# Linformer attention and an MLP mixer on one core: gated loads, reordered transposes, and stores on ScalarE's queue

## The chip, the cores and the metric

The kernel runs on one core of a Trainium2 chip. A core has a matrix engine (TensorE, in the profile PE; its weight loads are PEld), a vector engine (VectorE, DVE), an engine for activations (ScalarE, ACT), a general one (GpSimd, POOL) and SyncE (SP), which here only issues DMAs. Each engine works through its own instructions in order and waits at an instruction until the semaphores that it names are there. A DMA is issued by SP, ACT or POOL, and its data then move on DMA engines that all of them share. The metric is the device time of one execution in microseconds (us).

## What is computed

Eight batches, eight heads, 1024 positions, 64 values per head. Keys and values are first projected from 1024 positions to 64 (Linformer), then come scores, softmax and the weighted sum. The heads put side by side give x of 1024 x 512 per batch, which goes through a token-mixing and a channel-mixing MLP.

```python
k_proj = np.einsum('ks,bhsd->bhkd', E, k)          # E: 64 x 1024
v_proj = np.einsum('ks,bhsd->bhkd', F, v)
scores = scale * np.matmul(q, k_proj.transpose(0, 1, 3, 2))
attn = softmax(scores)
x = heads side by side of np.matmul(attn, v_proj)  # b, 1024, 512
h = np.maximum(x.transpose(0, 2, 1) @ w_tok1, 0.0) @ w_tok2   # 1024 -> 256 -> 1024
u = x + h.transpose(0, 2, 1)
h2 = np.maximum(u @ w_ch1, 0.0) @ w_ch2            # 512 -> 1536 -> 512
return u + h2
```

## The kernel before

All matrices are held in bf16; products are summed in f32 in PSUM. GpSimd loads q, k and v (f32 in memory) and casts them on the way (`load_kv` L79, `load_q` L87, two DMAs of 512 KB for each of q, k, v from batch 1 on). The tiles `k_sb`, `v_sb` and `q_sb` have two buffers each, so a batch's tiles are those of the batch two before.

The work of a batch has two parts. The *front* (`front_units`) is a list of steps: `kv_proj` (L176, L177), `k_transpose` (L191), four `scores` (matmuls L202, exp on ACT L207), eight `attend` (matmuls L214, division on DVE L221 and L222), two `token1` (L232, relu on ACT L236) and eight `token2` (L241, add on DVE L245, which gives `u_sb`). After the fourth and the eighth `token2`, SP transposes a half of `u_sb` by DMA into `uT` (L248). `token1` and `token2` share one PSUM buffer, so the next `token2` waits until DVE has read the last.

The *back* (`back_blocks`) is channel mixing, cut into 48 blocks of four matmuls. `ch1` (24 blocks, L347) makes a chunk `g_ps` of the hidden layer from `uT`, and ACT's relu puts it into `gT` (L351). `ch2` (24 blocks, L358; three make one output tile) sums `o2_ps` from `gT`, which the profile calls `o_ps` like that of `attend`; DVE adds `u_sb` (L365) into an output tile `o_sb`, one of four, and SP stores it (L366, 256 KB). `g_ps` and `o2_ps` take turns in the three PSUM banks of `psC`. Batch 0 runs all `ch1` before all `ch2`; the others go half by half: 12 `ch1`, 12 `ch2`, 12 `ch1`, 12 `ch2`.

A loop over the batches weaves the back of batch b with the front of batch b + 1: after each block as many steps are emitted as keep the two lists in proportion. Batches 0 and 1 transpose q on PE (L161, `qT` by ACT, L166). From batch 2 on SP transposes it by DMA, two of them per batch (`q_transpose`, L95), and that step stands in the middle of the steps of the loop before: the loop of batch b transposes q of batch b + 2. At the loop's start GpSimd copies one element of `gT` into `gate` (L398), and behind it in the source come the loads of batch b + 2.

The source's order is not binding. A scheduler puts every engine's instructions in an order of its own, as their dependences allow; the copy to `gate` and the loads behind it share no data. The profile's times are those of the order so found.

Of the kernel before, what the change touches and what calls it, by code (L numbers as in the profile page):

```python
# [15 lines left out]
def kernel(  # L16
# [13 lines left out]
    nc = tc.nc  # L30
    P = 128

    B, H, S, D = q.shape
# [18 lines left out]
    attn_pool = ctx.enter_context(tc.tile_pool(name="attn", bufs=4))  # L52
    mix_pool = ctx.enter_context(tc.tile_pool(name="mix", bufs=2))
    gT_pool = ctx.enter_context(tc.tile_pool(name="gT", bufs=2))
    out_pool = ctx.enter_context(tc.tile_pool(name="outp", bufs=4))
    psC = ctx.enter_context(tc.tile_pool(name="psC", bufs=3, space=bass.MemoryType.PSUM))
    psA = ctx.enter_context(tc.tile_pool(name="psA", bufs=2, space=bass.MemoryType.PSUM))
    psS = ctx.enter_context(tc.tile_pool(name="psS", bufs=1, space=bass.MemoryType.PSUM))
# [11 lines left out]
    def load_kv(b, parts):  # L70
        k_sb, v_sb, q_sb = [
            kv_pool.tile([P, H, NSI, D], BF16, tag=name, name=name) for name in ("k_sb", "v_sb", "q_sb")
        ]
        qT = mix_pool.tile([P, H, NJ, P], BF16, tag="qT", name="qT")
        loaded[b] = (k_sb, v_sb, q_sb, qT)
        hn = H // parts
        for h in range(0, H, hn):
            for t, src in ((k_sb, k), (v_sb, v)):
                nc.gpsimd.dma_start(  # L79
                    out=t[:, h : h + hn],  # L80
                    in_=src[b, h : h + hn].rearrange("h (p si) d -> p h si d", p=P),
                )

    def load_q(b, parts):
        hn = H // parts
        for h in range(0, H, hn):
            nc.gpsimd.dma_start(  # L87
                out=loaded[b][2][:, h : h + hn],
                in_=q[b, h : h + hn].rearrange("h (p si) d -> p h si d", p=P),
            )  # L90

    def q_transpose(b):
        q_sb, qT = loaded[b][2:]
        for h in range(0, H, H // 2):
            nc.sync.dma_start_transpose(  # L95
                out=qT[:, h : h + H // 2].rearrange("p h j s -> p (h j) s"),
                in_=q_sb[:, h : h + H // 2].rearrange("p h si d -> p (h si d)"),
            )

    load_kv(0, HP)  # L100
# [7 lines left out]
    for c in range(0, DC, DC // 4):  # L108
        nc.gpsimd.dma_start(
            out=wc1_sb[:, :, c : c + DC // 4],  # L110
            in_=moe_w_ch1.rearrange("(dc p) c -> p dc c", p=P)[:, :, c : c + DC // 4],
# [4 lines left out]
    for c in range(0, CC, CC // 4):  # L116
        nc.gpsimd.dma_start(
            out=wc2_sb[:, c : c + CC // 4],
            in_=moe_w_ch2.rearrange("(cc p) d -> p cc d", p=P)[:, c : c + CC // 4],
# [24 lines left out]
    def front_units(b):  # L144
# [189 lines left out]
        units += [lambda si=si: token2(si) for si in range(NSI)]  # L334
        return units

    out_v = out.rearrange("b (p si) d -> b p si d", p=P)

    def back_blocks(b):

        u_sb, uT = us.pop(b), uTs.pop(b)
        st = {}

        def ch1(i, cc):
            g_ps = psC.tile([P, S2], F32, tag="c", name="g_ps")
            for dc in range(DMC):
                nc.tensor.matmul(  # L347
                    g_ps, wc1_sb[:, dc, cc * P : (cc + 1) * P], uT[i][:, :, dc, :],
                    start=(dc == 0), stop=(dc == DMC - 1),
                )  # L350
            nc.scalar.activation(out=st["gT", i][:, cc, :], in_=g_ps, func=ACT.Relu)  # L351

        def ch2(i, ss, part):
            if part == 0:
                st["o"] = psC.tile([P, DM], F32, tag="c", name="o2_ps")
            o2_ps = st["o"]
            for cc in range(part * 4, part * 4 + 4):
                nc.tensor.matmul(  # L358
                    o2_ps, st["gT", i][:, cc, ss * P : (ss + 1) * P], wc2_sb[:, cc, :],
                    start=(cc == 0), stop=(cc == CC - 1),  # L360
                )
            if part == CC // 4 - 1:
                si = i * NJ + ss
                o_sb = out_pool.tile([P, DM], F32, tag="o_sb", name="o_sb")
                nc.vector.tensor_add(out=o_sb, in0=o2_ps, in1=u_sb[:, si, :])  # L365
                nc.sync.dma_start(out=out_v[b, :, si, :], in_=o_sb)  # L366

        def half(i):
            st["gT", i] = gT_pool.tile([P, CC, S2], BF16, tag="gT", name="gT")

        up, down = [], []
        for i in range(2):
            up.append([lambda i=i: (half(i), ch1(i, 0))])
            up[i] += [lambda i=i, cc=cc: ch1(i, cc) for cc in range(1, CC)]
            down.append(
                [lambda i=i, ss=ss, p=p: ch2(i, ss, p) for ss in range(NJ) for p in range(CC // 4)]
            )
        if b == 0:
            blocks = up[0] + up[1] + down[0] + down[1]
        else:  # L380
            blocks = up[0] + down[0] + up[1] + down[1]
        return blocks, lambda: st["gT", 0]

    gate = const.tile([1, 1], BF16, name="gate")
    rest = front_units(0)
    for b in range(B):
        blocks, first_tile = back_blocks(b)
        n0, n1 = 2, len(blocks) - 5
        if b == 0:
            for block in blocks[:16]:  # L390
                block()
                if rest:
                    rest.pop(0)()
        else:
            blocks[0]()
        if b + 2 < B:

            nc.gpsimd.tensor_copy(out=gate, in_=first_tile()[0:1, 0, 0:1])  # L398
            load_kv(b + 2, 2)
            load_q(b + 2, 2)  # L400
        if b == 0:
            blocks = blocks[16:]
            n0, n1 = 0, len(blocks) - 4
        else:
            blocks = blocks[1:]
        units = front_units(b + 1) if b + 1 < B else []
        if b + 2 < B:
            units.insert(len(units) // 2, lambda b=b: q_transpose(b + 2))
        done = 0
        for n, block in enumerate(blocks):  # L410
            block()
            want = max(0, n + 1 - n0) * len(units) // (n1 - n0)
            while done < min(want, len(units)):
                units[done]()
                done += 1


# [1 line left out]
_INS = ['q', 'k', 'v', 'E', 'F', 'moe_w_tok1', 'moe_w_tok2', 'moe_w_ch1', 'moe_w_ch2']  # L419
_OUTS = [((8, 1024, 512), 'float32')]  # L420
# [25 lines left out]
```

## Time and profile before

| | us |
|---|---|
| median of 3 runs | 499.16 |
| lowest, highest | 493.22, 503.42 |
| the profiled execution | 492.7 |
| its span, first to last instruction | 490.9 |
| PE busy in it | 453.0 (92%) |
| DVE, ACT, POOL busy | 176.1, 165.9, 50.0 |

The granted TensorE clock is 0.981 on average. A row of the profile names the line of the kernel, the engine and what the instruction writes and reads (`out<-in`, buffer numbers left out, or with one where there are several of a name). Of a DMA the row of the issuing queue (SPq, POOLq) shows how long it held the queue; "to landing" is from issue to the last byte.

### The profile page before, as it was taken

To read this page: it belongs to the slowest core of one execution; us is meant where nothing else is said; L and a number is where in the kernel's file an instruction comes from. 1 tells how busy PE (TensorE), PEld (TensorE's weight loads), DVE (VectorE), ACT (ScalarE), POOL (GpSimd) and SP (SyncE) were. 2 spreads that over 40 slices of the span, in tenths; PEclk is the share of its full clock that TensorE was granted. 3 is DMA by queue.
4 is the path that set the end of the run, shared out by engine and by line. 5 is a ranking of instruction groups with operands and counts; after the bars stand their busy time and mean duration, and the time that the engine had idled before them with its cause. 6 is when DMAs were issued, how large, how long until landed. Compare 5 with 4: busy or idle time off the path is not lost.

```text
span 490.9 us, 6248 instructions
## 1 busy us (share of the span) xinstructions
PE 453.0 (92%) x2588; PEld 220.6 (45%) x2624; DVE 176.1 (36%) x345; ACT 165.9 (34%) x259; POOL 50.0 (10%) x78
## 2 busy tenths in 40 slices
PE   2789999249999999999999999999999999999996
PEld 2566444014444444444444444444454434444442
DVE  3472224113361534332452525243351425241102
ACT  1257560002525053322524062422524061514150
POOL 7533320110210020100200020000000000000000
PEclk9999999678999999999999999999999999999999
DMA  8999999999895459924980559223010601033102
GB/s 127 207 204 206 206 206 197 202 210 229 141 203 86 99 121 210 170 43 131 163 181 1 122 120 210 64 64 108 22 65 0 160 12 65 21 87 85 65 21 85
DMA packets 93051, 60.43 MB, mean 123 GB/s; under 512 B 56160, under 2 KB 84320, under 8 KB 93024
## 3 DMA queue, kind: packets, MB, share of 16 engines
q0 software_dynamic: 29728, 29.63, 37.1%
q1 hardware_dynamic: 63296, 30.42, 25.3%
q8 instruction: 20, 0.33, 0.3%
q14 instruction: 7, 0.06, 0.0%
HBM read 59.24 MB, written 16.78 MB: 155 GB/s over the span
## 4 chain that ended last, share of the span: by engine, by line
PE 76%; DMA 16%; SPq 5%; issue 1%; POOL 0%; DVE 0%; POOLq 0%; DVEq 0%
PE o_ps L358 30%; PE g_ps L347 30%; DMA wc_sb<-in_moe_w_ch_dram 7%; DMA q_sb<-in_q_dram 6%; PE u_ps L241 5%; SPq L95 5%; PE h_ps L232 4%; DMA out_dram<-o_sb 2%; PE o_ps L214 2%; PE kv_ps L176 2%; PE s_ps L202 2%; DMA v_sb<-in_v_dram 1%; PE kt_ps L191 0%; DVE o_sb L365 0%; POOL k_sb L79 0%
## 5 line engine op out<-in xcount | busy, mean ns | idle before, releaser
L351 ACT ACTIVATE gT<-g_ps 128x512 bf16<-128x512 f32 x192 | 115.2, 600 | 232.9 <-PE g_ps L347 232.5
L358 PE MATMUL o_ps<-wc_sb,gT 128*128 128x512 bf16 x739 | 182.3, 382 | 1.6 <-issue 0.2
L347 PEld LDWEIGHTS <-wc_sb 128*128 128x128 bf16 x768 | 72.2, 98 | 84.5 <-issue 5.8
L358 PEld LDWEIGHTS <-gT 128*128 128x128 bf16 x768 | 72.5, 98 | 80.1 <-issue 6.3
L365 DVE TENSOR_TENSOR o_sb<-o_ps,u_sb 128x512 f32<-128x512 f32 x64 | 44.3, 692 | 85.4 <-PE o_ps L358 66.8
L245 DVE TENSOR_TENSOR u_sb<-u_ps,x_sb 128x512 bf16<-128x512 f32 x56 | 38.7, 692 | 92.7 <-PE u_ps L241 90.8
L241 PE MATMUL u_ps<-hT_sb,wt_sb 128*128 128x512 bf16 x111 | 34.3, 390 | 17.5 <-DVE u_sb L245 17.5
L222 DVE TENSOR_TENSOR x_sb<-o_ps,rdn 128x512 bf16<-128x512 f32 x64 | 44.3, 692 | 2.2
L207 ACT ACTIVATE a_sb<-s_ps 128x1024 bf16<-128x1024 f32 x32 | 32.9, 1032 | 29.6 <-PE s_ps L202 29.5
L221 DVE RECIPROCAL rdn<-o_ps 128x8 f32<-128x8 f32 x64 | 13.1, 205 | 68.2 <-PE o_ps L214 68.2
L181 DVE CAST kp_sb<-kv_ps 64x512 bf16<-64x512 f32 (+1 forms) x22 | 10.9, 532 | 54.3 <-PE kv_ps L177 54.3
L241 PEld LDWEIGHTS <-wt_sb 128*128 128x128 bf16 x112 | 16.2, 145 | 30.9 <-issue 21.8
L214 PEld LDWEIGHTS <-a_sb 128*128 128x128 bf16 x256 | 19.5, 99 | 16.5 <-DVE x_sb L222 3.2
L232 PE MATMUL h_ps<-x_sb,wt_sb 128*128 128x512 bf16 x106 | 26.1, 379 | 0.4
L87 POOL DMA_DIRECT2D q_sb<-in_q_dram x18 | 13.3, 739 | 85.8 <-DMA qT<-q_sb 75.4
L176 PE MATMUL kv_ps<-k_sb,ET_sb 128*64 128x512 bf16 (+1 forms) x88 | 18.3, 355 | 3.8 <-DMA k_sb<-in_k_dram 3.8
L177 PE MATMUL kv_ps<-v_sb,FT_sb 128*64 128x512 bf16 (+1 forms) x88 | 17.4, 354 | 3.1 <-DMA v_sb<-in_v_dram 3.1
L398 POOL COPY gate<-gT 1x1 bf16<-1x1 bf16 x6 | 1.1, 177 | 155.7 <-ACT gT L351 155.7
L232 PEld LDWEIGHTS <-wt_sb 128*128 128x128 bf16 x112 | 11.0, 98 | 13.2
L236 ACT ACTIVATE hT_sb<-h_ps 128x512 bf16<-128x512 f32 x14 | 8.4, 597 | 25.0 <-PE h_ps L232 25.0
L79 POOL DMA_DIRECT2D k_sb<-in_k_dram x18 | 13.5, 752 | 27.6 <-PE kv_ps L177 20.3
L214 PE MATMUL o_ps<-vb_134,a_sb 128*128 128x130 bf16 x128 | 12.8, 223 | 2.3 <-DVE x_sb L222 2.3
(67 smaller groups left out, 342.4 us busy)
## 6 DMA issues: line engine op xcount, KB each, us to landing
out_dram<-o_sb SPq DMA_DIRECT2D x64, 256.0 KB, 2.6
k_sb<-in_k_dram POOLq DMA_DIRECT2D x14, 512.0 KB, 9.7
v_sb<-in_v_dram POOLq DMA_DIRECT2D x14, 512.0 KB, 11.6
q_sb<-in_q_dram POOLq DMA_DIRECT2D x14, 512.0 KB, 11.4
wc_sb<-in_moe_w_ch_dram POOLq DMA_DIRECT2D x8, 384.0 KB, 16.2
k_sb<-in_k_dram POOLq DMA_DIRECT2D x4, 256.0 KB, 7.6
v_sb<-in_v_dram POOLq DMA_DIRECT2D x4, 256.0 KB, 8.2
q_sb<-in_q_dram POOLq DMA_DIRECT2D x4, 256.0 KB, 10.0
```

Of the source, the lines that this page charges most:

```text
L95: nc.sync.dma_start_transpose(out=qT[:, h : h + H // 2].rearrange("p h j s -> p (h j) s"), in_=q_sb[:, h : h + H // 2].rearrange("p h si d ...
L176: nc.tensor.matmul(kv_ps[0:KP], ET_sb[:, si, :], k_sb[:, hs, si, :], start=a, stop=z)
L207: nc.scalar.activation(out=a_sb, in_=s_ps, func=ACT.Exp, scale=scale)
L214: nc.tensor.matmul(o_ps[:, j // 2, (j % 2) * 2 * D1 : (j % 2 + 1) * 2 * D1], a_sb[:, h % 2, j * P : (j + 1) * P], vb[:, h // 2, h % 2].rea ...
L222: nc.vector.tensor_tensor(out=x_sb[:, :, h * D : (h + 1) * D].rearrange("p (n c) d -> p n c d", n=2), in0=o4[:, :, :, 0:D], in1=rdn[:, :, ...
L232: nc.tensor.matmul(h_ps, wt1_sb[:, si, t * P : (t + 1) * P], x_sb[:, si, :], start=(si == 0), stop=(si == NSI - 1),)
L241: nc.tensor.matmul(u_ps, wt2_sb[:, t, si::NSI], hT_sb[:, t, :], start=(t == 0), stop=(t == TC - 1),)
L245: nc.vector.tensor_add(out=u_sb[:, si, :], in0=u_ps, in1=x_sb[:, si, :])
L347: nc.tensor.matmul(g_ps, wc1_sb[:, dc, cc * P : (cc + 1) * P], uT[i][:, :, dc, :], start=(dc == 0), stop=(dc == DMC - 1),)
L351: nc.scalar.activation(out=st["gT", i][:, cc, :], in_=g_ps, func=ACT.Relu)
L358: nc.tensor.matmul(o2_ps, st["gT", i][:, cc, ss * P : (ss + 1) * P], wc2_sb[:, cc, :], start=(cc == 0), stop=(cc == CC - 1),)
L365: nc.vector.tensor_add(out=o_sb, in0=o2_ps, in1=u_sb[:, si, :])
```

## The change

- `load_ahead` issues the copy to `gate` and ties the loads of batch b + 2 behind it (`tc.issue_after`): they can't be put ahead of it. In loop 0 the copy stands where it stood, behind the first 16 blocks; in later loops behind the sixth block, and it reads the sixth chunk of `gT`.
- The two DMA transposes of q are kept in the source's order on SP (`tc.keep_in_program_order`) and are appended to the steps, behind the last `token2` and so behind both transposes of u, where they stood in the middle.
- A store is no longer issued by SP with its add. It is put on a list and issued by ACT after the next block and the steps behind that one (`flush`); the rest follow at the end.
- The output tile has five buffers for four.
- The loops from batch 1 on spread their steps over 42 blocks where it was 40, since their first block is now part of the list.

```diff
-    out_pool = ctx.enter_context(tc.tile_pool(name="outp", bufs=4))
+    out_pool = ctx.enter_context(tc.tile_pool(name="outp", bufs=5))
...
     def q_transpose(b):
         q_sb, qT = loaded[b][2:]
         for h in range(0, H, H // 2):
-            nc.sync.dma_start_transpose(
-                out=qT[:, h : h + H // 2].rearrange("p h j s -> p (h j) s"),
-                in_=q_sb[:, h : h + H // 2].rearrange("p h si d -> p (h si d)"),
+            tc.keep_in_program_order(
+                nc.sync.dma_start_transpose(
+                    out=qT[:, h : h + H // 2].rearrange("p h j s -> p (h j) s"),
+                    in_=q_sb[:, h : h + H // 2].rearrange("p h si d -> p (h si d)"),
+                )
             )
...
+    stores = []
+
+    def flush(n):
+
+        for dst, o_sb in stores[:n]:
+            nc.scalar.dma_start(out=dst, in_=o_sb)
+        del stores[:n]
...
-                nc.sync.dma_start(out=out_v[b, :, si, :], in_=o_sb)
+                stores.append((out_v[b, :, si, :], o_sb))
...
+    def load_ahead(b, cc):
+
+        if b + 2 < B:
+            passed = nc.gpsimd.tensor_copy(out=gate, in_=first_tile()[0:1, cc, 0:1])
+            with tc.issue_after(passed.ins):
+                load_kv(b + 2, 2)
+                load_q(b + 2, 2)
...
-        n0, n1 = 2, len(blocks) - 5
         if b == 0:
-            for block in blocks[:16]:
+            for n, block in enumerate(blocks[:16]):
                 block()
                 if rest:
                     rest.pop(0)()
-        else:
-            blocks[0]()
-        if b + 2 < B:
-
-            nc.gpsimd.tensor_copy(out=gate, in_=first_tile()[0:1, 0, 0:1])
-            load_kv(b + 2, 2)
-            load_q(b + 2, 2)
-        if b == 0:
+            load_ahead(0, 0)
             blocks = blocks[16:]
-            n0, n1 = 0, len(blocks) - 4
-        else:
-            blocks = blocks[1:]
+        n0, n1 = (0, len(blocks) - 4) if b == 0 else (2, len(blocks) - 4)
         units = front_units(b + 1) if b + 1 < B else []
         if b + 2 < B:
-            units.insert(len(units) // 2, lambda b=b: q_transpose(b + 2))
+            units.append(lambda b=b: q_transpose(b + 2))
         done = 0
         for n, block in enumerate(blocks):
+            made = len(stores)
             block()
+            if b > 0 and n == 5:
+                load_ahead(b, 5)
             want = max(0, n + 1 - n0) * len(units) // (n1 - n0)
             while done < min(want, len(units)):
                 units[done]()
                 done += 1
+            flush(made)
+    flush(len(stores))
```

Line numbers of the changed kernel are 1 to 10 higher, so L96 below is L95 before, L250 is L248, and a store is L344.

On SP, the first instructions of the program, which belong to loop 0, stood before like this (`qT` of batches 2 and 3, `uT` of batch 1, and the stores of batch 0):

```order
L95 DMA_TRANSPOSE qT<-q_sb 128x16x128 x2
L366 DMA out_dram<-o_sb 128x512
L95 DMA_TRANSPOSE qT<-q_sb 128x16x128 x2
L366 DMA out_dram<-o_sb 128x512 x4
L248 DMA_TRANSPOSE uT_728<-u_sb 128x16x128
L366 DMA out_dram<-o_sb 128x512 x2
L248 DMA_TRANSPOSE uT_729<-u_sb 128x16x128
```

And after the change, on SP from the same place on (`uT` of batch 1, `qT` of batch 2, then `uT` of batch 2):

```order
L250 DMA_TRANSPOSE uT_728<-u_sb 128x16x128
L250 DMA_TRANSPOSE uT_729<-u_sb 128x16x128
L96 DMA_TRANSPOSE qT<-q_sb 128x16x128 x2
L250 DMA_TRANSPOSE uT_1131<-u_sb 128x16x128
L250 DMA_TRANSPOSE uT_1132<-u_sb 128x16x128
```

The stores are gone from SP, the transposes of u stand ahead of those of q, and those of batch 3 have left loop 0.

On GpSimd, the difference between loop 0 and loop 1, behind the loads of batch 2 (with `q_sb` at its head):

```order
 L87 DMA q_sb<-in_q_dram 128x4x512 x2
-L79 DMA k_sb<-in_k_dram 128x4x512
-L79 DMA v_sb<-in_v_dram 128x4x512
-L79 DMA k_sb<-in_k_dram 128x4x512
-L79 DMA v_sb<-in_v_dram 128x4x512
-L87 DMA q_sb<-in_q_dram 128x4x512 x6
-L398 COPY gate<-gT 1x1
+L399 COPY gate<-gT 1x1
```

Keys and values of batch 3, and q of batches 3, 4 and 5, were issued ahead of the second copy to `gate`; now none is, and the six loads of batch 3 follow that copy.

On ACT, from the end of loop 0 to the first chunks of loop 1, the order after the change (before, the same rows stood without the stores):

```order
L238 ACTIVATE hT_sb<-h_ps 128x512
L344 DMA out_dram<-o_sb 128x512
L238 ACTIVATE hT_sb<-h_ps 128x512
L344 DMA out_dram<-o_sb 128x512 x4
L361 ACTIVATE gT<-g_ps 128x512 x8
```

The last four stores of batch 0 now stand right ahead of the relus of batch 1's first chunks, and the same place recurs at every half.

## The prediction

> **What bounds the kernel now.** I read the page's busy shares and its slices first, to see where TensorE (PE) is not at work.
>
> ```profile
> span 490.9 us, 6248 instructions
> ...
> PE   2789999249999999999999999999999999999996
> ...
> PEclk9999999678999999999999999999999999999999
> ```
>
> A slice is 490.9 / 40 = 12.3 us. After the start, PE is at nine tenths or more everywhere but in slices 8 and 9, from about 86 to 110 us; there the granted clock falls too. The table by stage puts numbers on that place, on the stages ahead of it and on two batches behind it.
>
> ```profile
> 43.70:73.80 30.10, 30.05 (x200) 14.37 (x199) 7.14 (x15) 20.31 (x31) 8.91 (x12) 1.00 1.24 206
> 73.80:87.70 13.90, 13.80 (x75) 7.00 (x76) 6.36 (x14) 1.20 (x2) 0.00 (x0) 1.00 1.29 193
> 87.70:117.75 30.05, 12.39 (x43) 5.15 (x43) 6.63 (x10) 0.00 (x0) 2.96 (x4) 0.72 1.20 210
> 117.75:172.49 54.74, 54.48 (x293) 25.61 (x297) 21.46 (x39) 19.08 (x30) 4.63 (x7) 1.00 0.72 144
> 172.49:227.07 54.58, 54.32 (x293) 25.51 (x296) 21.46 (x39) 19.08 (x30) 4.64 (x7) 1.00 0.69 136
> ```
>
> Columns: stage, its length, then busy time and count of PE, PE's weight loads, VectorE, ScalarE, GpSimd, granted clock, share of the DMA engines, GB/s. A whole batch behind the hole has 54.32 of 54.58 us of PE work: no schedule wins more than 0.3 us there. The stage 87.70 to 117.75 has 43 matmuls in 30.05 us. What they need is given by the chain of work that ended last, where PE runs unhindered:
>
> ```profile
> 172.49 4.32 PE g_ps L347 x20
> ```
>
> That is 4.32 / 20 = 0.216 us for a matmul of 512 columns, so 43 need 9.3 us and the stage loses 30.05 - 9.3 = 20.8 us. The rows of PE and of VectorE (DVE) in that window say what PE waited for:
>
> ```profile
> 97.64 1.01 PE L241 MATMUL u_ps<-hT_sb,wt_sb 128*128 128x512 bf16 x2 [9.75 <-DVE u_sb L245]
> ...
> 110.88 1.01 PE L241 MATMUL u_ps<-hT_sb,wt_sb 128*128 128x512 bf16 x2 [7.71 <-DVE u_sb L245]
> ...
> 96.29 0.69 DVE L365 TENSOR_TENSOR o_sb<-o_ps,u_sb 128x512 f32<-128x512 f32 x1 [9.92 <-DMA out_dram<-o_sb]
> ...
> 109.54 0.69 DVE L365 TENSOR_TENSOR o_sb<-o_ps,u_sb 128x512 f32<-128x512 f32 x1 [7.88 <-DMA out_dram<-o_sb]
> ```
>
> Two holes of 9.75 and 7.71 us, 17.5 us in all; the other 3.3 us of the 20.8 went while the clock stood at 0.72. Each time token mixing waits for DVE, and DVE for one of four output tiles whose store has not landed. The stores stand on SyncE's queue (SP):
>
> ```profile
> 73.77 17.24 SPq L95 DMA_TRANSPOSE qT<-q_sb  x1
> 91.05 0.58 SPq L366 DMA_DIRECT2D out_dram<-o_sb  x1
> 91.77 6.44 SPq L95 DMA_TRANSPOSE qT<-q_sb  x2
> 98.26 2.83 SPq L366 DMA_DIRECT2D out_dram<-o_sb  x4
> 101.69 9.65 SPq L248 DMA_TRANSPOSE uT_728<-u_sb  x1
> ...
> 54.88 18.87 DMA q_sb<-in_q_dram
> ...
> 98.26 11.19 DMA out_dram<-o_sb
> ```
>
> The last two rows are from the chain. Batch 2's q lands at 73.8; its second transpose then holds SP until 91.0 and batch 3's until 98.2, with the stores behind them in order. And DMA is full, because loads of later batches run beside the transposes:
>
> ```profile
> 67.52 0.75 POOL L87 DMA_DIRECT2D q_sb<-in_q_dram  x1 [2.93 <-issue]
> 68.89 0.74 POOL L87 DMA_DIRECT2D q_sb<-in_q_dram  x1 [0.62 <-DMA v_sb<-in_v_dram]
> 96.08 1.48 POOL L87 DMA_DIRECT2D q_sb<-in_q_dram  x2 [26.45 <-DMA qT<-q_sb]
> 109.03 1.48 POOL L87 DMA_DIRECT2D q_sb<-in_q_dram  x2 [11.48 <-DMA qT<-q_sb]
> ```
>
> These are q of batches 3, 4 and 5, far ahead of need.
>
> **The change part by part.** The durations of the moved steps, from the groups by line and the DMA issues (the three numbers are min/median/max in ns of holding the issuing queue; "to landing" is in us):
>
> ```profile
> L366 SPq DMA_DIRECT2D out_dram<-o_sb x64: 332/333/1487, 91.1 to 487.6; - x64
> ...
> DMA to landing us min/median/max: 2.0/2.6/11.2
> ...
> L95 SPq DMA_TRANSPOSE qT<-q_sb x12: 1337/2233/17241, 71.2 to 304.0; - x12
> ...
> qT<-q_sb SPq DMA_TRANSPOSE x12, 4.7
> uT_728<-u_sb SPq DMA_TRANSPOSE x1, 14.0
> ...
> uT_1150<-u_sb SPq DMA_TRANSPOSE x1, 4.3
> uT_1151<-u_sb SPq DMA_TRANSPOSE x1, 4.4
> ...
> L248 SPq DMA_TRANSPOSE uT_1150<-u_sb x1: 1838/1838/1838, 162.7 to 162.7; - x1
> L248 SPq DMA_TRANSPOSE uT_1151<-u_sb x1: 1318/1318/1318, 169.8 to 169.8; - x1
> ...
> 169.94 0.69 DVE L365 TENSOR_TENSOR o_sb<-o_ps,u_sb 128x512 f32<-128x512 f32 x1 [0.17 <-PE o_ps L358]
> ...
> L365 DVE TENSOR_TENSOR o_sb<-o_ps,u_sb 128x512 f32<-128x512 f32 x64 | 44.3, 692 | 85.4 <-PE o_ps L358 66.8 <-DMA out_dram<-o_sb 17.8 <-remote 0.8
> L351 ACT ACTIVATE gT<-g_ps 128x512 bf16<-128x512 f32 x192 | 115.2, 600 | 232.9 <-PE g_ps L347 232.5
> ```
>
> *Loads tied behind the gate.* Batch 2's loads stand where they stood. Batch 3's, which shared DMA with the transposes, now wait for the sixth channel-mixing chunk of batch 1. From then on a batch's six loads of 0.5 MB are one burst: 3.1 MB at the 206 GB/s of the stage from 43.7 take 15.3 us, and are used one loop (54.6 us) later. Cost zero, covered by that loop; if the cover failed, a loop could wait up to those 15.3 us.
>
> *Stores off SP, and a fifth tile.* With stores on ScalarE (ACT) no transpose stands ahead of them. At 2.6 us to landing, and with an output tile needed only each third block (3 x 4 x 0.216 = 2.6 us), five tiles bridge 13 us; even the slowest landing, 11.2 us, is covered. So both holes go: minus 20.8 us, the clock's part included.
>
> *u transposes ahead of q's.* The first transpose of u is now issued right after the fourth token-mixing step, with 38 matmuls (counted in PE's order, 8.2 us) before the first chunk that reads it: 0.2 + 0.7 (VectorE's add) + 4.3 to landing = 5.2 us, where the 0.2 is the 0.17 of the row at 169.94. It fits by 3 us. With 14.0 us to landing, as `uT_728` took among loads, it would be 6.7 us late.
>
> *q transposes last.* Behind the last token-mixing step there are 14 matmuls (3.0 us) to the next loop, then eight chunks of 4 and the key and value projection beside them (about 9 us) to the first scores: 12 us. The chain is 0.9 for the add, 1.3 for u's second transpose on SP, 2.2 for the first of q, 4.7 from the issue of the second: 9.1 us. Covered by 3 us, and the first scores need the first half alone.
>
> *What ACT pays.* 64 stores x 333 ns = 21 us of its idle time; it waits 232 us for PE in front of chunks alone. It matters where a store stands right ahead of a chunk's relu, once per half: o_ps is done, 0.2 + 0.69 for the add, 0.33 for the store, 0.6 for the relu, 1.8 us, where PE needs the bank back after three chunks, 2.6 us. It costs nothing by the median; with the slowest issue, 1.487 us, it would be 3.0 us, 0.4 late, and over 14 such places 5 us. ACT has issued no DMA before, so the ends are 0 and 5 us; I take 1, as nearly all of the 64 rows lie at the median.
>
> [...]
>
> *The interleave.* 25 steps spread over 42 blocks instead of 40, with as many blocks behind them: the same matmuls, with batches already full. Zero, but for rounding.
>
> **Sum.** The profiled execution took 492.7 us, 1.8 more than its span. 492.7 - 20.8 + 1 = **473 us**. It stands 6.5 below the median of the runs shown (499.16; 493.22 to 503.42). Where the slower runs lose theirs is not shown: if in the hole, it goes too; if elsewhere, the result is 479.
>
> **The rivals.** *The hole shrinks but stays.* Stores and u transposes issue early, yet share the DMA engines and land late. For it: the store of 98.26 took 11.19 us though it was already issued. Against it: loads ran beside that one, and now do not. Price: the first transpose of u late by up to 6.7 us, 473 + 6.7 = 480. [...]
>
> *ACT is held by SP's transposes.* At each loop's end four transposes hold SP for 1.8 + 1.3 + 2.2 + 2.2 us, with ACT's stores among them. If a store can't issue beside a transpose, the last one waits until 3.6 us after the loop's start (0.9 + 1.3 + 2.2 + 2.2 - 3.0), is out at 3.9, the relu done at 4.5, where PE needed 2.6: 1.9 us in each of six loops, 11 us, or 484 in all.
>
> *Slower: the burst of loads overtakes q's second transpose.* The gate opens at the sixth chunk: 24 matmuls, the projection (8 pairs at 0.216), relu and issue, about 8.6 us into the loop. That transpose lands at 1.4 + 4.7 = 6.1 us. Margin 2.5 us; once it is gone, the transpose runs under full loads, where one held SP for 17.2 us instead of 2.2: the third scores, some 12 us into the loop, wait about 10 us, six times: 60 us, 533 in all. It beats the gain from 3.5 us per loop on.
>
> *It does nothing*, 493: the tied order does not come about. The order of the changed program shows that it does.
>
> **How the numbers follow.** Forecast 0.70, hole stays 0.10, ACT held 0.12, slower 0.05, nothing 0.03. The forecast's own range is 470 (no cost on ACT, 2 us from elsewhere) to 479 (as above). The range goes over the 480 of the hole that stays up to the 484 of ACT held, and 2 us lower for scatter: 468 to 484 leaves out less than 2 in 10. A measurement of this kernel tells about 2% from no change; against 499.16 that is 489, against the profiled 492.7 it is 483, so I split ACT held, 0.05 faster and 0.07 same. Faster: 0.70 + 0.10 + 0.05 = 0.85; same: 0.07 + 0.03 = 0.10; slower: 0.05.
>
> **What would show it.** Right: PE at nine tenths in slices 8 and 9; no wait of VectorE's output add for a store; u's transposes landing in about 4.4 us; batch 1's first chunk at about 97 us instead of 117.75; loops of 54.6 us. Wrong: stores on ACT of over 1 us beside SP's transposes, with PE waiting for relus at a loop's start (ACT held); PE waiting for `uT` at about 97 us (hole stays); scores waiting for `qT`, loops of over 60 us (slower). Wrong too if PE stalls ahead of 87 us, where the loads of the start are unchanged.

## The result, and the profile after

| | before | after |
|---|---|---|
| median, us | 496.43 (4 runs, 493.22 to 503.42) | 472.32 (4 runs, 471.89 to 472.96) |
| the profiled execution and its span, us | 492.7, 490.9 | 472.96, 471.2 |

The ratio is 0.9536, 95% interval 0.9455 to 0.9616: faster, by 4.6%. It compares the means of the executions within 1.5% of the fastest of their kernel, so the one at 503.42, in a slower state, is left out. The forecast was 473.0 (468 to 484). The page of the changed kernel, its slices of 11.8 us:

```profile
span 471.2 us, 6248 instructions
...
PE   2789999999999999999999999999999999999996
...
PEclk9999999999999999999999999999999999999999
```

PE is at nine tenths or more in every slice between the start and the last one, and the clock no longer falls. The table by stage (columns as in the prediction: stage, its length, then busy time and count of PE, PE's weight loads, VectorE, ScalarE, GpSimd, granted clock, share of the DMA engines, GB/s) begins at the same 87.70 us as before and is cut where batch 1's first chunk of channel mixing starts, and at the two loops behind it:

```profile
87.70:98.46 10.76, 10.62 (x48) 5.15 (x48) 6.33 (x10) 0.00 (x0) 0.00 (x0) 1.00 0.48 113
98.46:152.97 54.51, 54.25 (x293) 25.54 (x297) 21.17 (x39) 18.93 (x30) 4.64 (x7) 1.00 0.71 141
152.97:207.47 54.50, 54.24 (x293) 25.48 (x297) 21.16 (x39) 18.93 (x30) 4.64 (x7) 1.00 0.70 136
```

The stage with the holes took 30.05 us and takes 10.76, with no idle time to speak of. The first chunk starts at 98.46 instead of 117.75, 19.29 us earlier. The loops are 0.1 to 0.2 us shorter, and from the first chunk to the end the kernel needs 471.2 - 98.46 = 372.7 us where it needed 490.9 - 117.75 = 373.2. One more thing stands between the two profiles: the same chain of batch 0's chunks starts later in the second one, as these two rows of PE show (before, then after):

```profile
44.71 6.21 PE L347 MATMUL g_ps<-uT_172,wc_sb 128*128 128x512 bf16 x28
```

```profile
45.89 6.21 PE L357 MATMUL g_ps<-uT_172,wc_sb 128*128 128x512 bf16 x28
```

That is 1.2 us. It is scatter of the start and not the change: batch 0's first chunk starts at 37.62 us in the profile before and at 38.81 in this one, but at 37.0 to 38.2 in four profiles of the kernel before, and at 37.4 in two of the kernels below that lack only one part of the change. So the account of the spans is: the holes -20.5, the later start +1.2, the rest -0.4, together -19.7.

What SP does at the place of the holes, from its timeline after the change:

```profile
90.86 1.38 SPq L250 DMA_TRANSPOSE uT_728<-u_sb  x1
96.36 2.31 SPq L250 DMA_TRANSPOSE uT_729<-u_sb  x1
98.84 6.26 SPq L96 DMA_TRANSPOSE qT<-q_sb  x2
```

The transposes of u hold SP for 1.4 and 2.3 us where the first held it for 9.65. The transposes of q begin at 98.84, where the first began at 71.2, and are off SP by 105.1. The loads of batch 3 are issued behind them, as GpSimd's timeline shows. The second transpose, issued at 103.30, lands at 107.65, 0.6 us after the first of these loads is issued, and PE's third scores of the loop, the first to read the second half of `qT`, find it there:

```profile
106.52 0.18 POOL L399 COPY gate<-gT 1x1 bf16<-1x1 bf16 x1 [50.05 <-ACT gT L361]
107.03 0.74 POOL L79 DMA_DIRECT2D k_sb<-in_k_dram  x1 [0.34 <-issue]
```

```profile
111.34 0.41 PE L204 MATMUL s_ps<-qT,kT 64*64 64x512 bf16 x4
```

The stores on ACT, and q's transposes on SP (min/median/max of holding the queue, in ns):

```profile
L344 ACTq DMA_DIRECT2D out_dram<-o_sb x64: 338/338/375, 71.7 to 467.8; - x64
...
DMA to landing us min/median/max: 2.0/3.5/6.7
```

```profile
L96 SPq DMA_TRANSPOSE qT<-q_sb x12: 1801/3806/4362, 98.8 to 373.7; - x12
...
DMA to landing us min/median/max: 4.3/6.0/8.5
```

No store takes ACT longer than 0.375 us. The transposes of q hold SP longer than the prediction's 2.2 us, and land 6.0 us after issue instead of 4.7; more on that below.

### The profile page after: what moved, and what is told of

Same layout as the page of the kernel before. It is cut to its first block, busy times and chain, and to the rows that moved or that the text cites. A ratio compares the mean times of both kernels' runs of the same rounds, so it can differ in the third digit from the quotient of the medians.

```text
span 471.2 us, 6248 instructions
## 1 busy us (share of the span) xinstructions
PE 451.5 (96%) x2588; PEld 221.8 (47%) x2624; DVE 175.0 (37%) x345; ACT 165.0 (35%) x259; POOL 50.1 (11%) x78
## 3 DMA queue, kind: packets, MB, share of 16 engines
q1 hardware_dynamic: 54080, 13.63, 16.7%
## 4 chain that ended last, share of the span: by engine, by line
PE 93%; DMA 4%; DVE 1%; POOL 1%; issue 1%; POOLq 0%
PE g_ps L357 36%; PE o_ps L368 35%; PE u_ps L243 5%; PE h_ps L234 5%; PE o_ps L216 3%; PE kv_ps L178 3%; PE s_ps L204 2%; DMA q_sb<-in_q_dram 2%; DMA k_sb<-in_k_dram 1%; PE up_ps L271 1%; PE t_ps L163 1%; PE hp_ps L260 1%; DVE x_sb L224 1%; PE kt_ps L193 1%; PE ut_ps L281 0%
## 5 line engine op out<-in xcount | busy, mean ns | idle before, releaser
L243 PE MATMUL u_ps<-hT_sb,wt_sb 128*128 128x512 bf16 x107 | 32.2, 378 | 0.1
L243 PEld LDWEIGHTS <-wt_sb 128*128 128x128 bf16 x112 | 16.1, 144 | 12.2 <-issue 2.6
L178 PEld LDWEIGHTS <-ET_sb 128*64 128x64 bf16 x88 | 8.9, 129 | 12.5 <-issue 7.7
L168 ACT COPY qT<-t_ps 128x1024 bf16<-128x1024 bf16 x8 | 8.2, 1030 | 18.1 <-PE t_ps L163 18.1
## 6 DMA issues: line engine op xcount, KB each, us to landing
v_sb<-in_v_dram POOLq DMA_DIRECT2D x14, 512.0 KB, 11.8
```

The source lines that it names most:

```text
L178: nc.tensor.matmul(kv_ps[0:KP], ET_sb[:, si, :], k_sb[:, hs, si, :], start=a, stop=z)
L243: nc.tensor.matmul(u_ps, wt2_sb[:, t, si::NSI], hT_sb[:, t, :], start=(t == 0), stop=(t == TC - 1),)
```

## The experiments

The change has three parts that can be made alone: the loads tied behind the gate (L), the stores on ACT with the fifth tile (S), and the transposes of q last and in order (Q). Two small ones, the later place of the gate and the steps spread over more blocks, belong to none of these: they are left out of the kernels with one part alone, and stay in those less one part. The first runs put each alone into the kernel before, the next ones take each alone out of the changed kernel, and the last ones move the gate and shorten the loads' packets.

### The loads alone

```diff
-            nc.gpsimd.tensor_copy(out=gate, in_=first_tile()[0:1, 0, 0:1])
-            load_kv(b + 2, 2)
-            load_q(b + 2, 2)
+            passed = nc.gpsimd.tensor_copy(out=gate, in_=first_tile()[0:1, 0, 0:1])
+            with tc.issue_after(passed.ins):
+                load_kv(b + 2, 2)
+                load_q(b + 2, 2)
```

> The kernel before with one edit: the loads of batch b + 2 are tied behind the copy to the gate, which stays where it was. Stores stay on SyncE behind the q transposes, four output tiles. Theory A (the hole needs two things at once, q's transposes ahead of the stores on SyncE and loads of later batches beside them, so that taking away either closes it): q of batch 2 is transposed in about 2 us a piece from 73.8 us on, the stores go out by 78 us, no wait for an output tile of over 1 us, 470 to 476 us. Theory B (the order on SyncE alone is the cause: stores must leave its queue): the holes stay at 10 us or more, 485 to 495 us. Theory C (the full DMA engines alone are the cause): as A, 470 to 476 us.

Measured: 472.2 us against 493.24 of the kernel before on the same chip, ratio 0.9558 (0.9512 to 0.9604). SP's timeline and the group of q's transposes:

```profile
71.15 5.86 SPq L95 DMA_TRANSPOSE qT<-q_sb  x2
77.05 10.20 SPq L366 DMA_DIRECT2D out_dram<-o_sb  x5
90.45 1.99 SPq L248 DMA_TRANSPOSE uT<-u_sb  x1
```

```profile
L95 SPq DMA_TRANSPOSE qT<-q_sb x12: 1317/1718/2738, 71.1 to 337.1; - x12
```

The transposes of batch 2's q stand at the same place as before, ahead of the stores on the same queue, and hold SP for 5.86 us, no single one for more than 2.74, where one held it for 17.24. The loads beside the transposes are gone (the DMA engines' share from 73.8 to 87.7 us is 0.55, before 1.29). The order on SP also changed in one point, since batch 3's q is now loaded later: its two transposes, which held SP for 6.44 us in loop 0, have moved to loop 1 (116.47 us). The whole gain is there, with the stores still on SP behind the transposes of batch 2's q, so Theory B falls.

### The stores alone

```diff
-    out_pool = ctx.enter_context(tc.tile_pool(name="outp", bufs=4))
+    out_pool = ctx.enter_context(tc.tile_pool(name="outp", bufs=5))
...
-                nc.sync.dma_start(out=out_v[b, :, si, :], in_=o_sb)
+                stores.append((out_v[b, :, si, :], o_sb))
```

with `flush` on ACT as in the change.

> The kernel before with one edit: stores issued by ScalarE after the next block, five output tiles. Loads and q transposes as before, so on SyncE four q transposes (batches 2 and 3) now stand ahead of the first u transpose, with loads beside them. Theory A: no wait for an output tile any more, but the first u transpose is issued only at about 98 us and lands at 105 to 112 us, so TensorE stops at about 97 us for batch 1's first chunk: a hole of 8 to 15 us in another place, 479 to 489 us. Theory B (stores must leave SyncE, and that is all): 470 to 476 us. Theory C (full DMA engines): stores and transposes both late, 488 to 495 us.

Measured: 501.43 us, ratio 1.0133 (1.0076 to 1.019): slower than before by about 1%. That is less than the 2% that count as a change, but all four executions (500.13 to 501.59) lie above all seven of the kernel before on that chip (492.68 to 497.54). All three theories were too low, and Theory A, which named the place, has its mechanism right: the hole doesn't merely stay, it grows. SP, the chain of waits, and PE:

```profile
71.40 31.99 SPq L95 DMA_TRANSPOSE qT<-q_sb  x4
103.50 20.60 SPq L248 DMA_TRANSPOSE uT<-u_sb  x2
```

```profile
73.88 19.64 SPq L95
93.65 7.74 SPq L95
101.43 1.97 SPq L95
103.50 20.93 DMA uT<-u_sb
```

```profile
124.47 1.86 PE L354 MATMUL g_ps<-uT,wc_sb 128*128 128x512 bf16 x4 [26.14 <-DMA uT<-u_sb]
```

The two waits for output tiles are gone, and one wait of 26.14 us for `uT` stands in their place. The transposes of u still queue on SP behind four transposes of q, the first two of them amid the loads (a share of 1.19 from 73.8 to 87.7 us); and when u's turn comes at 103.5, the next loads of q have just been set free by the transposes of q, as GpSimd shows:

```profile
102.28 1.48 POOL L87 DMA_DIRECT2D q_sb<-in_q_dram  x2 [32.73 <-DMA qT<-q_sb]
```

So u's transposes crawl too: the first takes 20.9 us to landing. The run also shows what a store on ACT does while one transpose holds SP for 19.64 us: the five stores issued in that time hold ACT for 0.34 to 0.40 us, and of all 64 none holds it longer than 0.773.

### q's transposes last, alone

```diff
-            units.insert(len(units) // 2, lambda b=b: q_transpose(b + 2))
+            units.append(lambda b=b: q_transpose(b + 2))
```

and `keep_in_program_order` around them, as in the change.

> The kernel before with one edit: the q transposes are kept in order and stand behind the last token-mixing step, so behind five stores and both u transposes on SyncE. Loads run ahead as before (keys, values and q of batch 3 right behind batch 2's), stores stay on SyncE, four output tiles. Theory A: stores go out as they are made and the loads of batch 3 are over by about 90 us, 470 to 477 us. Theory B: as the stores stay on SyncE the hole stays, 485 to 495 us. Theory C: loads still fill the DMA engines at 74 to 90 us and stores land in about 11 us, holes of 5 us or more, 480 to 495 us.

Measured: 473.07 us, ratio 0.9566 (0.9522 to 0.9611). SP:

```profile
72.23 17.30 SPq L368 DMA_DIRECT2D out_dram<-o_sb  x5
91.35 1.91 SPq L250 DMA_TRANSPOSE uT<-u_sb  x1
...
98.36 6.21 SPq L96 DMA_TRANSPOSE qT<-q_sb  x2
```

Here the loads stay as free as in the kernel before (the DMA engines' share from 73.8 to 87.7 us is 1.21, before 1.29), but hardly a transpose runs beside them: the last of batch 3's loads lands at 91.9, 0.6 us after the first transpose of u is issued, those of q begin at 98.36, and the loads that reuse `q_sb` can't start before q has been transposed. This is a second way to the whole gain. It also rules out that the full DMA engines alone make the holes (Theory C): the five stores of 72 to 90 us, beside the same loads, landed after 3.4 to 6.2 us, and no output tile was waited for.

### The changed kernel less one part

With q's transposes back in the middle (L and S left):

> The changed kernel with the q transposes put back into the middle of the steps (loads tied, stores on ScalarE). Theory A (what costs is a transpose beside loads of later batches, whatever stands behind it): q of batch 2 is transposed at 74 to 79 us with no loads beside it, the u transposes land in about 5 us, 471 to 474 us. Theory D (stores on ScalarE cost time whenever q's transposes stand ahead of u's, as in the run with that edit alone): 480 us or more.

With the stores back on SP (L and Q left), which is the one line

```diff
-            nc.scalar.dma_start(out=dst, in_=o_sb)
+            nc.sync.dma_start(out=dst, in_=o_sb)
```

> The changed kernel with the stores given back to SyncE, still after the next block and with five tiles (loads tied, q transposes last). Theory A: no transpose runs beside loads, so the stores behind it wait a few us at most: 471 to 474 us. Theory B (stores must leave SyncE): 485 us or more.

Without the tie (S and Q left):

> The changed kernel without the tie: loads may run ahead of the gate again (stores on ScalarE, q transposes last). Theory A: keys, values and q of batch 3 run from 74 to about 90 us and are over when the first u transpose is issued at 91 us, 471 to 475 us; were they later, that transpose would be hit and the time 480 to 500 us. Theory C (loads beside anything on the DMA engines are the cause): 480 us or more.

Measured, against 492.38 on that chip: 472.29 (ratio 0.9598, 0.9497 to 0.9699), 471.86 (0.9589, 0.9548 to 0.963) and 472.16 (0.9595, 0.9539 to 0.9651). So the theories with 480 us or more fall in all three. Without the tie batch 3's loads were not quite over when they were expected to be: the last lands at 93.2 us, and the first transpose of u, issued at 89.5 beside it, still landed after 5.5 us. All eight combinations, in us:

| | neither L nor Q | L | Q | L and Q |
|---|---|---|---|---|
| stores on SP | 493 | 472.2 | 473.1 | 471.9 |
| stores on ACT | 501.4 | 472.3 | 472.2 | 472.3 |

Either of L and Q brings all of it, both bring no more, and the stores on ACT bring nothing beside either and lose 8 us without. (The kernels less one part ran twice each; the executions of the six that have L or Q lie between 471.2 and 473.9.) What L and Q have in common is that batch 2's transposes of q no longer run beside loads, and that batch 3's have left loop 0. No run takes away one without the other, so how the 20.5 us divide between them isn't shown; in the profile before, batch 2's second transpose held SP for 17.24 us and batch 3's two for 6.44.

The stores on ACT have a small price that stays hidden. With the stores on SP, the DMA issues of the changed kernel less S:

```profile
out_dram<-o_sb SPq DMA_DIRECT2D x64, 256.0 KB, 2.9
...
qT<-q_sb SPq DMA_TRANSPOSE x12, 4.5
```

A transpose of q lands in 4.5 us there and in 6.0 with the stores on ACT, a store in 2.9 and in 3.5. The other three pairs go the same way (q's transposes by the median: 4.7 and 6.8 with neither L nor Q, 4.6 and 5.9 with L, 5.4 and 6.2 with Q). With the stores on SP, the first store behind the transposes of q at the start of loop 1 (they hold SP from 96.51 to 102.72 us) is issued at 102.83. In the changed kernel one moved at the same time as they did: issued by ACT at 99.38, amid the first transpose of q (98.84 to 104.98), it landed after 3.2 us.

### The gate too early

The prediction's slower rival was that the burst of loads overtakes q's second transpose. The next run makes it happen: the gate of loops 1 to 5 at the first chunk instead of the sixth.

```diff
-            if b > 0 and n == 5:
-                load_ahead(b, 5)
+            if b > 0 and n == 0:
+                load_ahead(b, 0)
```

> The changed kernel with the gate of loops 1 to 5 opened at the first chunk instead of the sixth, so that the burst of loads begins 5 to 7 us earlier, at about 2 us into the loop, when q's second transpose has just been issued. This is the prediction's slower rival made to happen. Theory A: the second transpose is caught by the loads and lands up to 20 us after its issue instead of 6; the third scores wait for it, 2 to 10 us in each of five loops, 482 to 520 us. Rival: the transpose has moved most of its data before the loads arrive, no wait of TensorE for it, 471 to 474 us.

Measured: 538.65 us, ratio 1.0947 (1.0852 to 1.1041). PE's waits, and its scores in loop 1:

```profile
PE s_ps L204 <- DMA qT<-q_sb: 55.7, 7, 12.2
```

```profile
108.77 0.41 PE L204 MATMUL s_ps<-qT,kT 64*64 64x512 bf16 x4 [1.65 <-DMA qT<-q_sb]
...
122.74 0.64 PE L204 MATMUL s_ps<-qT,kT 64*64 64x512 bf16 x4 [10.41 <-DMA qT<-q_sb]
```

The third scores wait 9.1 to 12.2 us in each of loops 1 to 5. The mechanism is that of the prediction, and so is the price of one loop (10 us). That its 533 came near has some luck in it: it counted six loops, and loads come behind the gate in five; their waits are 53.9 us, and the rest goes with a lower clock, 0.94 on average over the span. Between this kernel and the changed one stand five chunks in the place of one instruction, and 66 us (538.65 - 472.3). The kernel with L alone has its gate at the first chunk too, without harm. It is L and Q together that need the later gate: they put the loads and the transposes of q next to each other at the start of a loop.

The next run looks for the edge: the gate at the fourth chunk.

> The changed kernel with the gate of loops 1 to 5 at the fourth chunk of channel mixing instead of the sixth, so that the loads begin some 7 us earlier (two chunks of 3.6 us) and their data come to the DMA engines while q's second transpose is still under way. Theory A (what counts is whether the transposes' packets share the engines with the loads' packets before the third scores at about 111 us ask for them): q's second transpose, held until about 105 us, is caught for its last part only, 472 to 485 us; a wait of the third scores on qT of up to 2 us per loop. Rival (the margin is so wide that the place of the gate does not matter until the loads come ahead of the first transpose): 471 to 474 us and no wait on qT.

Measured: 479.65 us (2 runs, 478.56 and 480.75); the kernel before took 497.7 on that chip, ratio 0.9637 (0.9551 to 0.9723). GpSimd and PE:

```profile
103.16 0.74 POOL L79 DMA_DIRECT2D k_sb<-in_k_dram  x1 [0.34 <-issue]
```

```profile
115.69 0.64 PE L204 MATMUL s_ps<-qT,kT 64*64 64x512 bf16 x4 [4.47 <-DMA qT<-q_sb]
```

The first load is issued 3.9 us earlier than in the changed kernel (7 were expected), 2.3 us before q's second transpose leaves SP. That transpose lands 12.6 us after its issue instead of 4.3, and the third scores of loop 1 wait 4.47 us, in loop 3 0.79; the other loops don't wait. The span of this profile is 479.0 us, 7.8 over that of the changed kernel; 5.3 of these are the two waits. The time is in the range of Theory A, though the expected up to 2 us in every loop were one larger wait instead. So the gate of the changed kernel could open earlier without harm by less than 3.9 us.

The prediction had a margin of 2.5 us, from the landing of q's second transpose to the first load. That margin was not there: in loops 1 to 5 of the changed kernel the transpose lands within 0.7 us of the issue of the first load, before or after it (loop 1: 107.65 and 107.03). No scores waited, since they need it 3.7 us or more after its landing.

### Why a transpose beside loads is slow

Counting the packets of the two queues in the kernel before, while the second transpose of batch 2's q held SP (74 to 91 us; columns: packets, MB, share of 16 engines):

```profile
q0 software_dynamic: 2600, 2.58, 93.3%
q1 hardware_dynamic: 2337, 0.59, 30.3%
```

GpSimd's loads (q0) and SP's transposes (q1) got nearly as many packets through, 1.1 to 1; but a load's packet has 2.58 MB / 2600 = 990 bytes and a transpose's 250. So the transposes had 0.59 of 3.17 MB. Such counts would come about if an engine took its packets from the two queues by turns, whatever their length; these counts alone don't show that it does. If it does, shorter packets of the loads must make the transpose faster with as many bytes moved. So the kernel with the gate at the first chunk was run again with the loads from batch 3 on cut by halves of the positions instead of halves of the heads:

```diff
+                    nc.gpsimd.dma_start(
+                        out=t[:, :, s : s + NJ],
+                        in_=src[b].rearrange("h (p si) d -> p h si d", p=P)[:, :, s : s + NJ],
+                    )
```

> The kernel with the gate at the first chunk (538.65 us), with the loads of the batches from the fourth on cut so that each piece is contiguous for half as many bytes: the same number of DMAs and bytes, smaller packets. Theory A (each DMA engine serves the queues packet by packet, so that a transpose of small packets waits a load's packet for each of its own): half the packet, half the wait; 490 to 515 us and q's transposes landing in 12 to 15 us at most instead of 22.5. Rival (a queue's share is one of time or bytes and does not depend on the packet's size): 530 to 550 us and landings of about 22 us.

Measured: 518.96 us (518.74 and 519.17; the kernel before 497.7, ratio 1.0427, 1.0352 to 1.0502). The queues from 96 to 125 us, with the long packets and then with the short ones, and PE's waits in the latter:

```profile
q0 software_dynamic: 3168, 3.15, 70.8%
q1 hardware_dynamic: 6240, 1.57, 38.6%
```

```profile
q0 software_dynamic: 5828, 2.94, 80.1%
q1 hardware_dynamic: 6240, 1.57, 39.5%
```

```profile
PE s_ps L204 <- DMA qT<-q_sb: 34.2, 7, 7.5
```

The rival, a share that doesn't depend on the packets, had 530 to 550 and falls. The wait fell from 55.7 to 34.2 us, to 0.61 of it. Half was expected, and both numbers of Theory A were missed: 515 by 4 us, and the slowest landing of q's transposes, 12 to 15 us expected, was 17.6 (22.5 with the long packets). A reason may be in the time of one load packet, 29 us x 16 engines x share / count: 0.104 us with the long and 0.064 us with the short ones, so a packet of half the bytes takes 0.61 of the time and not half. An estimate from these: a transpose is 2080 packets (54080 on SP's queue for 26 transposes in the changed kernel), 130 on each of 16 engines if they are spread evenly; if each waits for one load packet, the short ones save 130 x 0.040 = 5.2 us. The second transposes of loops 1 to 5 landed after 20.9 us on average with the long packets and after 16.4 with the short ones, 4.5 us less.

### The spread of the kernel before

The prediction left open where the longer executions (497 to 503 us) of the kernel before lose their time. It was profiled again, unchanged, three times:

> The kernel before, unchanged, for a second profile of it. If the spread of its runs (493 to 503 us) comes from the hole, then the length of the stage between 87 us and batch 1's first chunk differs from the 30.05 us of the first profile by as much as the whole time does, and all later batches take 54.6 us in both. If it comes from elsewhere, that stage is the same within 1 us.

> The kernel before, unchanged, profiled once more, in search of an execution among the longer ones (495 to 503 us), since the prediction left open where those lose their time. Theory A: in or ahead of the same hole (first chunk of batch 1 later than the 117.75 us of the first profile by what the execution is longer, loops behind it of 54.6 us). Rival: in the loops behind the hole (54.6 us each become 55 or more), which no part of the change would touch. An execution at 493 us tells nothing.

> The same once more, in case the third profile falls on a short execution. Theory A: what the execution takes over 492.7 us stands ahead of the first chunk of batch 1. Rival: it stands in the loops behind.

The three took 493.92, 499.34 and 493.61 us; the first and the last tell nothing of the longer ones. The second, from 87.70 us on, and PE's row at its first chunk:

```profile
87.70:121.60 33.90, 12.30 (x42) 5.17 (x42) 7.33 (x11) 0.00 (x0) 2.96 (x4) 0.73 1.28 175
121.60:179.14 57.54, 57.54 (x297) 26.32 (x297) 20.76 (x38) 19.08 (x30) 4.62 (x7) 0.95 0.75 144
179.14:233.70 54.56, 54.56 (x297) 25.52 (x296) 21.44 (x39) 19.08 (x30) 4.62 (x7) 1.00 0.67 136
```

```profile
121.60 7.27 PE L347 MATMUL g_ps<-uT,wc_sb 128*128 128x512 bf16 x20 [4.09 <-DMA uT<-u_sb]
```

Its span is 497.6, 6.7 us over the first profile's. The first chunk starts at 121.60 instead of 117.75, 3.9 us later, since it waits for `uT` as well: the first transpose of u took 20.3 us to landing, where it took 14.0 in the first profile; why it took longer this time isn't shown. The loop behind it takes 57.54 us instead of 54.74, 2.8 us more, at a clock of 0.95; the next loop is as ever. So this execution loses its 6.7 us in the same hole and in the loop behind it. That the change takes the spread away is likely and not shown: no kernel with L or Q scatters by more than 2.3 us, but several of them ran only twice, and the one with the stores alone, which has the hole, scatters by 1.5. It is one execution; the one at 503.42 has no profile.

## Why the prediction was right, point by point

- *The sum.* Predicted 492.7 - 20.8 + 1 = 473; the profiled execution took 472.96. The hole was worth 20.5 us, 0.3 less than predicted. The price on ACT, taken as 1 us between 0 and 5, was not there: with the rest of the kernel 0.4 us shorter, nothing can be put down to it. A later start of 1.2 us made up for both, so the last digit is luck. The signs came as named: no output add waits for a store, the loops take 54.5 us, and the first chunk starts at 98.46 us, 97 but for the later start.
- *Which part earns it.* Here the prediction was wrong, though its time was right. It booked the whole 20.8 us under "Stores off SP, and a fifth tile" and gave "Loads tied behind the gate" a cost of zero. Stores off SP alone lose 8 us; the loads alone, or q's transposes last alone, gain all 21. The time is right because the parts that were given no gain were changed along with it. The failed step is the sentence that with stores on ACT no transpose stands ahead of them, "so both holes go": it followed the holes to the queue in which the stores stood, and not on to what held that queue. The row was there, a transpose that held SP for 17.24 us where others took 2.2, with the loads beside it, and the prediction itself named them. What the runs put in its place: with the loads tied, and nothing else changed in the source, no transpose of q held SP for more than 2.74 us, and the holes were gone with the stores still on SP behind them. The prediction also had the price of what would be late next: `uT` 6.7 us late if u's transposes ran among loads. In the stores-alone kernel they wait their turn too, and the wait was 26.14 us.
- *u's transposes ahead of q's.* Issued at 90.86 and needed at 98.46: landed after 4.7 us by the table of DMA issues, so with 2.9 us to spare, as predicted (3 us).
- *q's transposes last.* Predicted 2.2 us on SP and 4.7 to landing, measured 3.8 and 6.0. The source of the difference is the stores that now move beside them: with these on SP they land in 4.5. So the chain of 9.1 us, from the last token-mixing step (95.6) to the landing of q's second half (107.65), took 12.0, and of the 3 us of cover before the first scores (107.86) 0.2 were left. What saved it is the sentence behind the sum: the first scores need the first half alone, and that landed at 104.98, 2.9 us ahead.
- *The interleave.* It cost nothing, as predicted. The steps were spread over 41 blocks before, not 40 (n1 - n0 = 43 - 2).
- *The rivals.* The hole that stays: no wait for `uT` is left in the changed kernel; but it is what the stores alone lead to, with the loads and not the stores beside the transposes. ACT held by SP's transposes: no run shows such a hold, nor the 11 us priced for it. A store held ACT for 338/338/375 ns in the changed kernel, and for no more than 0.773 us in the one with the stores alone, whose transposes of q held SP for 32 us. Slower by the overtaking loads: it did not come, though the margin of 2.5 us was used up, and where it was made to come it cost 66 us where 60 were predicted.
- *The range.* Its upper part was for the spread of the runs before (479) and for ACT (484). The only longer execution with a profile loses in the hole and in the loop behind it, which speaks against the 479 without settling it.

## What to carry to other kernels

When an engine waits for a queue, look at why the instruction at the queue's head takes long before moving what stands behind it: here the moved stores only left the next one in line to wait. Here the transposes of q, whose packets had 250 bytes, landed after 4.3 to 6.0 us with the loads tied and after up to 21.8 in the kernel before, where loads ran beside them; holding the loads back and moving the transposes behind them came out the same, and one of the two was enough. Made together, they needed a third step, the later gate. The gate that orders loads behind these transposes had an edge: two chunks earlier cost about 7 us, five chunks 66, so it is worth measuring how far such a gate stands from it.

## What the runs showed of the hardware

- While a transpose held SP beside loads in the kernel before (74 to 91 us), the queue of the loads got 2600 packets of 990 bytes through and that of the transposes 2337 of 250: nearly as many packets, less than a quarter of the bytes (0.59 MB to 2.58). With the gate at the first chunk, loads in packets of half the length cut the waiting for transposes to 0.61 of it (55.7 to 34.2 us).
- A 512 KB transpose landed in 4.2 us at best and in up to 27.8 beside loads, and held its issuing queue for 1.3 us at best and for up to 19.6. In both of the longest cases another transpose ahead of it was still moving: the first of q landed at 90.0 us and the second let go of SP at 91.0 in the kernel before, at 92.6 and 93.5 with the stores alone. Stores issued by another engine in those 19.6 us held their own queue for 0.34 to 0.40.
- The transposes of q, issued by SP, landed after 4.5 us by the median with the stores on SP too and after 6.0 with the stores on ACT, in kernels otherwise alike.
